# Attention followed by a gated FFN on one Trainium2 core: the two FFN layers interleaved, or in two phases with the gated values kept in DRAM between them

## The chip, the core and the metric

One core of a Trainium2 chip runs the whole kernel. The metric is the device time of one execution in microseconds (us). Engines are TensorE (PE; its weight loads are listed apart as PEld), VectorE (DVE), ScalarE (ACT), GpSimd (POOL) and SyncE (SP), which issues nearly all DMAs and issues them in order.

## What is computed

```python
# q, k, v: [B=4, H=8, S=768, D=64] float32; n_global = 8, n_local = 96
scores = q @ k.T / sqrt(D) + bias        # bias: -slope[head] * distance
scores = where(is_global | is_local, scores, -1e9)   # 8 first keys, 96 keys back
a = exp(scores - max); a = a / (a.sum(-1) + 1e-9)
x = (a @ v).transpose(0, 2, 1, 3).reshape(3072, 512)
h = x @ w_in                             # 512 x 2048
g = h * (1 / (1 + exp(-h)))
out = g @ w_out                          # 2048 x 512
```

The weights w_in and w_out lie in DRAM as float64.

## The kernel before

**Attention.** There are 24 blocks i of 128 query rows (6 per batch), each with 4 head pairs. A block loads k, q and v (L433, 256 KB each) and the 104 keys before it (L440, L443), turns k and q on TensorE (L448), computes the scores (L532 with whole float32 operands in the first 6 blocks, L508 with stacked high and low parts after that), softmax on VectorE and ScalarE (L547, L555, L562 to L571), turns the probabilities (L580), and multiplies them with v (L600, L614). The first blocks turn the result in one step more (L636). x is kept as a high and a low part, xh and xl (L645, L648), so that the FFN's products are three matmuls each: high times high, high times low, low times high.

**The FFN.** Two blocks i make a group g of 256 tokens; there are 12 groups. The hidden width is cut into 16 blocks f of 128. For each g and f:

- `moe_h`, the first layer: 12 matmuls of 128x256 (L763), 3 for each of 4 pieces c of the model width.
- `moe_tanh` on ScalarE (L769) and `moe_gate` on VectorE (L773) make the gated value th, 128x256 in float32. `moe_high` (ScalarE, L777) and `moe_low` (VectorE, L781) split it into gh and gl.
- `moe_o`, the second layer: 6 matmuls of 128x512 (L788), 3 for each of 2 token tiles tt, added up over the 16 f in one PSUM bank for each tt. After the last f, `moe_end` (L798, L800) halves the sum into osb and `moe_out` (L806) stores it.

**The weights.** 32 tiles n, each 512 KB of float64, alternate: n even is w_in for block f = n/2, n odd w_out for the same f. `stage` loads one, three VectorE steps (`conv1` to `conv3`, L368, L374, L380) put a float32 together out of the two words, ScalarE rounds it to the high part (`conv_hi`, L387), and VectorE subtracts (`conv_lo`, L391). All 32 tiles stay in SBUF in both parts (WIH, WIL, WOH, WOL, the last two of w_out in w_last); while those two are not yet filled they serve as staging buffers for eight of the loads (`lent`).

**The exponent scan.** All 32 tiles are loaded a second time (`stage` with the name c), and `check` reduces the exponents of each to a least and a greatest value (L411, two reductions for each tile). At the end they and a few other conditions are judged (`judge`, `verdict`, `keep`), and where one fails a general kernel runs after the fast one. A scan's load waits until four reductions before it are done, and for a first-layer block of the FFN: block 34 + 4n, counted over all groups.

**What sets the order.** Each operation is entered in a planner (`Plan`, L48 to L167) with its engine, an expected cost, a rank, what it depends on and which buffers it takes. `run` simulates all engines and lets each, whenever it is free, take the operation of the lowest rank that is ready and has room in the buffers. The order in which the operations were taken is then written out as the program of each engine, and nothing is reordered afterwards. PSUM's 8 banks are shared out by kind: at any time a table `own` in `room` keeps some banks for each kind, and `hold` says which of its three rows applies. `PAR` (L29 to L39) holds the costs and ranks. Where the planner has TensorE idle within its first 60 us (`WEND`=60000 ns), it puts in a filler: one matmul of 128x256 on a tile of zeros, whose result nobody uses (L899). For the ranks: attention's head pair u = 4i + hp has rank u; a weight tile has C0 + CR·n, its load LW less; all FFN matmuls have ranks over 1000, so that they fill up what attention leaves. In the order that results the second layer of group g stands between the first-layer blocks of group g + 1, one `moe_o` for each `moe_h`, from the start to the end.

Of the kernel before, what the change touches and what calls it, by code (L numbers as in the profile page):

```python
# [10 lines left out]
F32 = mybir.dt.float32  # L11
# [36 lines left out]
class Plan:  # L48
# [122 lines left out]
def attn_moe(ctx, tc, q, k, v, n_global, n_local, w_in, w_out, out):  # L171
# [23 lines left out]
    psum = ctx.enter_context(tc.tile_pool(name="psum", bufs=1, space=PSUM))  # L195

# [5 lines left out]
    NLAST = 2  # L202
    WOH = const.tile([P, NFC - NLAST, DM], F32R, name="WOH")
    WOL = const.tile([P, NFC - NLAST, DM], F32R, name="WOL")
    last_w = []

    def w_o(i, f):

        if f < NFC - NLAST:
            return (WOH, WOL)[i][:, f]  # L210
        if not last_w:
            last_w.extend(
                const.tile([P, NLAST, DM], F32R, name=f"w_last{x}", tag=f"last{x}") for x in range(2)
            )
        return last_w[i][:, f - (NFC - NLAST)]
# [76 lines left out]
    def bias_of(first, hp):  # L292
# [17 lines left out]
        big=3, qkn=3, vn=2, vp=2, KH=2, KL=2, QH=2, QL=2, pe=3, pt=2, xh=2, xl=2, mid=3, th=2, gh=2, gl=2,  # L310
# [34 lines left out]
    def weights(n, parts=True):  # L345

        f, o = divmod(n, 2)
        fs = slice(f * P, (f + 1) * P)
        if o:
            src = w_out.bitcast(U32).rearrange("(c p) (m w) -> c p m w", p=P, w=2)[f]  # L350
            return (src, w_o(0, f), w_o(1, f)) if parts else (src,)
        src = w_in.bitcast(U32).rearrange("(c p) (f w) -> p c f w", p=P, w=2)[:, :, fs]
        return src, WIH[:, :, fs], WIL[:, :, fs]

    def lent(n):
        return n % 5 - 3 if n < PAR["NX"] and n % 5 > 2 else None

    def stage(n, nm):
        if nm == "w" and lent(n) is not None:
            x = const.tile([P, 512, 2], U32, name=f"wl_{n}", tag=f"last{lent(n)}")  # L360
        else:
            x = sb3.tile([P, 512, 2], U32, name=f"{nm}_{n}", tag="big")
        st[nm, n] = x
        nc.sync.dma_start(x if n % 2 else x.rearrange("p (c f) w -> p c f w", c=NCC), weights(n, False)[0])

    def conv1(n):
        st["f", n] = f = sb2.tile([P, 512], U32, name=f"wf_{n}", tag="mid", bufs=5)
# [10 lines left out]
    def conv3(n):  # L378
        f = st["f", n]
        nc.vector.scalar_tensor_tensor(  # L380
            f, st["w", n][..., 1], 0xC0000000, f, ALU.bitwise_and, ALU.bitwise_or
        )
        f = f.bitcast(F32)
        st["f", n] = f if n % 2 else f.rearrange("p (c f) -> p c f", c=NCC)

    def conv_hi(n):
        nc.scalar.copy(weights(n)[1], st["f", n])  # L387

    def conv_lo(n):
        _, hi, lo = weights(n)  # L390
        nc.vector.tensor_sub(lo, st["f", n], hi.bitcast(F32))  # L391

    o_w, o_l = [], [None, None]
    for n in range(2 * NFC):
        rank = PAR["C0"] + PAR["CR"] * n
        a, m, x = [] if lent(n) is not None else [Buf("big")], Buf("mid"), lent(n)
        o = op("DMA", 1456, rank - PAR["LW"], (lambda n=n: stage(n, "w")), [o_l[x]] if not a else (), a, PAR["DW"])
        o = op("DVE", 335, rank, (lambda n=n: conv1(n)), [o], [*a, m])
        o = op("DVE", 602, rank, (lambda n=n: conv2(n)), [o], [*a, m])
        o = op("DVE", 602, rank, (lambda n=n: conv3(n)), [o], [*a, m])  # L400
        if x is not None:
            o_l[x] = o
        o_wf = o
# [252 lines left out]
    for i in range(B * NJ):  # L656
# [12 lines left out]
        for nm in "kq" if i else "":  # L669
# [97 lines left out]
    def moe_tanh(g, f):  # L767
        mo["th", g, f] = th = sb2.tile([P, GT], F32, name="th")
        nc.scalar.activation(th, mo["ph", g, f], AF.Tanh, scale=0.5)  # L769
# [4 lines left out]

    def moe_high(g, f):
        mo["gh", g, f] = gh = sb2.tile([P, GT], F32R, name="gh")
        nc.scalar.copy(gh, mo["th", g, f])  # L777

    def moe_low(g, f):
        mo["gl", g, f] = gl = sb2.tile([P, GT], F32R, name="gl")  # L780
        nc.vector.tensor_sub(gl, mo["th", g, f], mo["gh", g, f].bitcast(F32))  # L781

    def moe_o(g, f, tt, po):
        gh, gl, po = mo["gh", g, f], mo["gl", g, f], bank(po)
# [23 lines left out]
    o_h = {}  # L808
    FIRST = -1e6
    for g in range(NGRP):  # L810
        po = [Buf("po"), Buf("po")]
        last = [None, None]
        o = o_h[g - 1, NFC - 1] if g > 1 else None
        for f in range(NFC):
            rank = 1e3 + (max(g, 1) * NFC + f + (PAR["LAG"] + 0.5 if g else 0))
            ph, th, gh, gl = Buf("h"), Buf("th"), Buf("gh"), Buf("gl")
            for c in range(NCC):
                o = op("PE", 329, rank + PAR["LK"] / 10, (lambda g=g, f=f, c=c, h=ph: moe_h(g, f, c, h)),
                       [o, *o_w[2 * f]] + o_x[g], [ph, xb[g]["xh"], xb[g]["xl"]])
                if f == c == 0:  # L820
                    o["hold"] = 2 if g == 1 else 1
            o_h[g, f] = o
            t = op("ACT", 264, FIRST + rank, (lambda g=g, f=f: moe_tanh(g, f)), [o], [ph, th])
            t = op("DVE", 335, FIRST + rank, (lambda g=g, f=f: moe_gate(g, f)), [t], [ph, th])
            hi = op("ACT", 307, FIRST + rank, (lambda g=g, f=f: moe_high(g, f)), [t], [th, gh])
            lo = op("DVE", 335, FIRST + rank, (lambda g=g, f=f: moe_low(g, f)), [hi], [th, gh, gl])
            for tt in range(NB):
                last[tt] = op("PE", 651, rank, (lambda g=g, f=f, tt=tt, x=po[tt]: moe_o(g, f, tt, x)),
                              [hi, lo, last[tt], *o_w[2 * f + 1]], [gh, gl, *po[tt:]])
                if g < 2 and f == NFC - 1:  # L830
                    last[tt]["hold"] = 1
        ob = Buf("big")
        for tt in range(NB):
            parts = (0, 1) if g == NGRP - 1 and tt == NB - 1 else (None,)
            for h in parts:
                eng = "ACT" if tt % 2 and not h else "DVE"
                o = op(eng, dict(ACT=478, DVE=598)[eng] // len(parts), FIRST + rank,
# [4 lines left out]
    for u, o in o_s.items():  # L842
        g, m = divmod(u, NB * NHP)
        f = (g - 1) * NFC + m * NFC // (NB * NHP) - PAR["AHEAD"]
        if f >= 2 * NFC:
# [229 lines left out]
```

## Time and profile before

| | |
|---|---|
| two runs | 725.86 and 727.01 us, median 726.43 |
| span of the profiled execution | 724.9 us |
| DMA packets | 117499, 63.95 MB, mean 88 GB/s |
| HBM read, written | 56.69 MB, 6.29 MB |
| TensorE clock granted, by 40 slices of the span | 9 tenths or more in each |

The profile is of one execution. The span runs from the first to the last instruction of the program; the run's own device time is not shown for that execution, so the table sets the span beside the two runs. The busy time of TensorE counts matmuls that overlap, since the next one starts before the one ahead has ended; what a matmul costs in a dense row is the distance from its start to the next one's start. Rows of grouped instructions name the line, the engine, the operation, output and inputs, and after the bar the busy time, the mean of one in ns, and the idle time of the engine just before them with what ended most of it.

### The profile page before, as it was taken

The page shows a single profiled execution, that of the slowest core. Times are in us where ns is not written, and L with a number is a line of the kernel's source. Part 1 is how long each engine was busy: PE and PEld are TensorE (multiplying, and loading weights), DVE is VectorE, ACT ScalarE, POOL GpSimd, SP SyncE. Part 2 cuts the span into 40 slices and gives each one's busy share as a digit, 9 for nine tenths or more (in the row PEclk, how much of TensorE's full clock was granted, in tenths as well). Part 3 has the DMA queues.
Part 4 walks back from the last instruction along what each step waited for, and adds up shares of the span by engine and source line. Part 5 has one row for each costly group of instructions (what it writes and reads, how often), then busy time and mean ns, then how long its engine had stood idle before and what let it go on. Part 6 is the DMA issues. An engine that isn't in the chain of part 4 may idle for free.

```text
span 724.9 us, 13945 instructions
## 1 busy us (share of the span) xinstructions
PE 715.0 (99%) x5142; PEld 640.5 (88%) x5142; DVE 463.5 (64%) x1403; ACT 420.6 (58%) x1105; POOL 24.9 (3%) x81
## 2 busy tenths in 40 slices
PE   8999999999999999999999999999999999999996
PEld 5889899888999999998999999999899989998995
DVE  3599999767666667466666665665766666543332
ACT  5897444587557567566565565664755655543321
POOL 2000000000000000000000000000000000000000
PEclk9999999999999999999999999999999999999999
DMA  7888645043225123143142240421422412000000
GB/s 154 214 240 247 192 131 172 2 117 101 59 57 143 45 71 97 48 114 103 30 114 81 64 114 23 122 72 44 132 59 57 127 32 57 30 1 1 30 1 33
DMA packets 117499, 63.95 MB, mean 88 GB/s; under 512 B 93744, under 2 KB 110384, under 8 KB 117424
## 3 DMA queue, kind: packets, MB, share of 16 engines
q1 hardware_dynamic: 116992, 62.86, 32.2%
q8 instruction: 42, 0.69, 0.4%
q14 instruction: 33, 0.27, 0.1%
q10 hardware_dynamic: 432, 0.13, 0.1%
HBM read 56.69 MB, written 6.29 MB: 87 GB/s over the span
## 4 chain that ended last, share of the span: by engine, by line
PE 97%; DVE 1%; DMA 1%; ACT 1%; issue 0%; SPq 0%; ACTq 0%
PE bank L763 38%; PE bank L788 37%; PE bank L580 5%; PE bank L600 4%; PE bank L508 4%; PE bank L448 3%; PE bank L614 3%; PE bank L532 2%; DMA qn<-in_q_dram 1%; PE bank L899 0%; PE bank L636 0%; ACT pe L555 0%; DVE osb L800 0%; ACT osb L798 0%; DVE xl L648 0%
## 5 line engine op out<-in xcount | busy, mean ns | idle before, releaser
L763 PE MATMUL bank<-xh,WIH 128*128 128x256 f32 x768 | 223.6, 291 | 0.0
L763 PE MATMUL bank<-xl,WIH 128*128 128x256 f32 x768 | 216.2, 282 | 0.3 <-DVE xl L648 0.3
L763 PE MATMUL bank<-xh,WIL 128*128 128x256 f32 x768 | 214.8, 280 | 0.0
L763 PEld LDWEIGHTS bank<-xh,WIH 128*128 128x128 f32 x768 | 144.5, 188 | 9.8 <-issue 2.8
L763 PEld LDWEIGHTS bank<-xl,WIH 128*128 128x128 f32 x768 | 144.6, 188 | 6.8 <-DVE xl L648 0.5
L763 PEld LDWEIGHTS bank<-xh,WIL 128*128 128x128 f32 x768 | 144.8, 189 | 0.0
L788 PE MATMUL bank<-WOH,gh 128*128 128x512 f32 x336 | 135.9, 405 | 0.0
L777 ACT CAST gh<-th 128x256 fp32r<-128x256 f32 x192 | 77.3, 403 | 96.0 <-PE bank L788 68.6
L788 PE MATMUL bank<-WOH,gl 128*128 128x512 f32 x336 | 132.4, 394 | 0.0
L788 PE MATMUL bank<-WOL,gh 128*128 128x512 f32 x336 | 131.9, 393 | 0.0
L769 ACT ACTIVATE th<-bank 128x256 f32<-128x256 f32 x192 | 73.8, 384 | 94.4 <-PE bank L763 83.2
L773 DVE SCALAR_TENSOR_TENSOR th<-th,bank 128x256 f32<-128x256 f32 x192 | 80.5, 419 | 60.9 <-ACT th L769 59.1
L781 DVE TENSOR_TENSOR gl<-th,gh 128x256 fp32r<-128x256 f32 x192 | 81.5, 425 | 55.9 <-ACT gh L777 52.7
L547 DVE CUSTOM_DVE_ANT_0 pe<-bank,B 128x232 f32<-128x232 f32 (+1 forms) x192 | 69.0, 377 | 67.2 <-PE bank L508 55.7
L555 ACT ACTIVATE pe<-pe,NM 128x232 f32<-128x232 f32 (+1 forms) x192 | 90.2, 471 | 20.3 <-DVE NM L547 18.8
L586 ACT COPY pt<-bank 128x512 f32<-128x512 f32 (+1 forms) x96 | 52.6, 549 | 46.9 <-PE bank L580 46.8
L788 PEld LDWEIGHTS bank<-WOH,gl 128*128 128x128 f32 x336 | 63.0, 188 | 15.2
L788 PEld LDWEIGHTS bank<-WOL,gh 128*128 128x128 f32 x336 | 63.4, 189 | 6.3
L788 PEld LDWEIGHTS bank<-WOH,gh 128*128 128x128 f32 x336 | 63.4, 189 | 6.3 <-issue 0.3
L580 PE MATMUL bank<-ident,pe 128*128 128x128 f32 (+1 forms) x352 | 54.3, 274 | 0.6 <-DVE pe L571 0.6
L580 PEld LDWEIGHTS bank<-ident,pe 128*128 128x128 f32 (+1 forms) x352 | 42.0, 138 | 7.3 <-ACT xh L645 0.8
L411 DVE TENSOR_REDUCE TOP<-c 128x1 f32<-128x512 int16 x64 | 42.3, 680 | 0.4 <-DMA c<-in_moe_w_in_dram 0.4
(115 smaller groups left out, 899.2 us busy)
## 6 DMA issues: line engine op xcount, KB each, us to landing
c<-in_moe_w_in_dram SPq DMA_DIRECT2D x16, 512.0 KB, 4.7
c<-in_moe_w_out_dram SPq DMA_DIRECT2D x16, 512.0 KB, 4.7
vn<-in_v_dram SPq DMA_DIRECT2D x24, 256.0 KB, 4.0
w<-in_moe_w_in_dram SPq DMA_DIRECT2D x12, 512.0 KB, 4.4
w<-in_moe_w_out_dram SPq DMA_DIRECT2D x12, 512.0 KB, 4.2
kn<-in_k_dram SPq DMA_DIRECT2D x23, 256.0 KB, 3.0
qn<-in_q_dram SPq DMA_DIRECT2D x23, 256.0 KB, 3.1
out_dram<-osb SPq DMA_DIRECT2D x23, 256.0 KB, 3.1
```

What stands on the lines that cost most here:

```text
L411: nc.vector.tensor_reduce(TOP[:, i, n:n + 1], top, AX.X, (ALU.min, ALU.max)[i], apply_absolute_value=True)
L508: nc.tensor.matmul(ps[:, a, :n], t[x][:, hp], t[K[a]][:, hp, w0:], start=not m, stop=m == 1)
L547: nc.vector.tensor_tensor_reduce(t["p", hp][:, a, :n], t["s", hp][a][:, :n], B1[:, h] if i % NJ else B0[:, h], -SC, 3.0e38, ALU.add, ALU.m ...
L555: nc.scalar.activation(x, x, AF.Exp, bias=NM[:, i * H + h:i * H + h + 1], scale=-1.0, accum_out=t["sum", hp][:, a:a + 1],)
L580: nc.tensor.transpose(ps[:n, c, a], pe[:, a, c0:c0 + n], ident)
L586: nc.scalar.copy(t["pt", hp][:, c], t["tp", hp][:, c])
L763: nc.tensor.matmul(ph, w[:, c, fs], x[:, c], start=not c and not n, stop=c == NCC - 1 and n == 2)
L769: nc.scalar.activation(th, mo["ph", g, f], AF.Tanh, scale=0.5)
L773: nc.vector.scalar_tensor_tensor(gf, gf, 1.0, mo["ph", g, f], ALU.add, ALU.mult)
L777: nc.scalar.copy(gh, mo["th", g, f])
L781: nc.vector.tensor_sub(gl, mo["th", g, f], mo["gh", g, f].bitcast(F32))
L788: nc.tensor.matmul(po, a[:, s], w_o(w, f), start=f == 0 and n == 0, stop=f == NFC - 1 and n == 2)
```

## The change

The two layers are split in two loops. In the first, all groups' `moe_h`, tanh and gate are entered, and each gated value, 128 KB, is written to DRAM (`moe_put`, L777, 192 of them on SP's queue). In the second, all groups' `moe_o` follow; their gated values are fetched back, two f at a time (`moe_get`, L781, 256 KB, 96 of them, each let go by the second layer six blocks ahead, GA=6, the first ones by the last blocks of the first layer), and `moe_high` (L785) and `moe_low` (L789) work on two f at once, so 96 of each where there were 192.

With it go:

- Weights: all of w_in first (n < 16), with ranks from 8 on (C0) and loads 12 ahead of that (LW); w_out after it with rank 8 + 5·(n - 16), so spread over the time of attention. The w_in tiles are staged in the buffers of the w_out tiles, which are not yet filled (tags wo0 to wo15): eight for the loads and eight for the float32 words, so a w_in tile from the ninth on waits for the conversion of the one eight before it.
- Scans: a scan's load waits for a second-layer block, 12 + 5n, instead of a first-layer one, so all 32 lie in the second phase.
- PSUM: `own` has other numbers, and the row with hold 2 begins at the second phase. `HU`, the head pair at which row 1 begins, is 9 instead of 13.
- The planner's costs of FFN matmuls are 355 and 700 ns instead of 329 and 651 (for three matmuls each), that of a w_in load 2000 instead of 1456.

```diff
-    CAP=dict(po=4, av=2, s=4, h=3, tp=2, tq=4), HU=13,
-    C0=14, CR=1, LW=1, LB=5, QB=3.5, RI=0.1, RN=0, RP=0.2, RM=0, RV=1.2, RQ=0.1, RB=3, LK=-25, LAG=1,
-    BP=(4, 3), NX=20, CF=2, AHEAD=5, CN=4, I0=6, IV=6, QS='ACT',
+    CAP=dict(po=4, av=2, s=4, h=3, tp=2, tq=4), HU=9,
+    C0=8, CR=1, LW=12, LB=5, QB=3.5, RI=0.1, RN=0, RP=0.2, RM=0, RV=1.2, RQ=0.1, RB=3, LK=-25, LAG=1,
+    BP=(4, 3), CF=12, AHEAD=5, CN=5, I0=6, IV=6, QS='ACT', O0=2, ON=5, GA=6, PF=16,
...
     def stage(n, nm):
-        if nm == "w" and lent(n) is not None:
-            x = const.tile([P, 512, 2], U32, name=f"wl_{n}", tag=f"last{lent(n)}")
+        if nm == "w" and n < NFC:
+            x = const.tile([P, 512, 2], U32, name=f"ws_{n}", tag=f"wo{HF + n % HF}")
...
+    def moe_put(g, f):
+        if g not in gate:
+            gate[g] = dram.tile([P, NFC, GT], F32, name=f"gate{g}")
+        nc.sync.dma_start(gate[g][:, f], mo["th", g, f])
+
+    def moe_get(g, f):
+        mo["g", g, f] = x = sb2.tile([P, 2, GT], F32, name="gx", tag="mid", bufs=5)
+        nc.sync.dma_start(x, gate[g][:, f:f + 2])
+
     def moe_high(g, f):
-        mo["gh", g, f] = gh = sb2.tile([P, GT], F32R, name="gh")
-        nc.scalar.copy(gh, mo["th", g, f])
+        mo["gh", g, f] = gh = sb2.tile([P, 2, GT], F32R, name="gh", tag="QH")
+        nc.scalar.copy(gh, mo["g", g, f])
...
+    for g in range(NGRP):
+        o = o_h[g - 1, NFC - 1] if g else None
+        for f in range(NFC):
+            rank = 1e3 + g * NFC + f
+            ph, th = Buf("h"), Buf("g1")
+            for c in range(NCC):
+                o = op("PE", 355, rank, (lambda g=g, f=f, c=c, h=ph: moe_h(g, f, c, h)),
+                       [o, *o_w[f]] + o_x[g], [ph, xb[g]["xh"], xb[g]["xl"]])
...
+            o_put[g, f] = op("DMA", 364, FIRST + rank, (lambda g=g, f=f: moe_put(g, f)), [t], [th], PAR["DO"])
+
     for g in range(NGRP):
...
-            rank = 1e3 + (max(g, 1) * NFC + f + (PAR["LAG"] + 0.5 if g else 0))
...
+            rank = 1e4 + g * NFC + f
+            if not f % 2:
+                gx = Buf("pt")
+                at = g * NFC + f - PAR["GA"]
+                o_g = op("DMA", 728, rank, (lambda g=g, f=f: moe_get(g, f)),
+                         [o_put[g, f], o_put[g, f + 1], o_h[NGRP - 1, max(at + NFC, 0)] if at < 0 else o_o[at]], [gx], PAR["DL"])
...
     for n, o in enumerate(o_cd):
-        g, f = divmod(2 * NFC + PAR["CF"] + PAR["CN"] * n, NFC)
-        plan.after(o, o_h[g, f])
+        plan.after(o, o_o[PAR["CF"] + PAR["CN"] * n])
```

By the two orders, three places look like this. The first is TensorE around the first FFN matmul. Before, the scores of 15 head pairs (L532, two matmuls each) stand ahead of it, and right before it turns of a block's result (L636) and of probabilities (L580):

```order
L532 MATMUL bank_83<-KHw,QHw 128x232
L532 MATMUL bank_88<-KHw,QHw 128x232
L636 MATMUL bank_82<-ident,xq 128x128 x4
L580 MATMUL bank_87<-ident,pe 104x128 x2
L580 MATMUL bank_87<-ident,pe 128x128 x2
L763 MATMUL bank_84<-xh,WIH 128x256
L763 MATMUL bank_84<-xl,WIH 128x256
L763 MATMUL bank_84<-xh,WIL 128x256
L532 MATMUL bank_85<-KHw,QHw 128x232
```

In the change, with the last of a row of fillers ahead of it (L918 is the old L899, L531 the old L532, L762 the old L763):

```order
L918 LDWEIGHTS wx
L918 MATMUL bank_88<-wx 128x256
L531 MATMUL bank_87<-KHw,QHw 128x232
L531 MATMUL bank_85<-KHw,QHw 128x232
L531 MATMUL bank_82<-KHw,QHw 128x232
L531 MATMUL bank_83<-KHw,QHw 128x232
L762 MATMUL bank_89<-xh,WIH 128x256
L762 MATMUL bank_89<-xl,WIH 128x256
L762 MATMUL bank_89<-xh,WIL 128x256
```

The first FFN matmul has moved ahead of attention's work: the scores of 10 head pairs stand ahead of it, and 56 fillers (27 of 28 before), twelve of them in a row.

The second place is SP's queue from its sixth row on, in the first 10 us. Before, there are only loads for attention:

```order
L433 DMA kn<-in_k_dram 128x8x64
L433 DMA qn<-in_q_dram 128x8x64
L433 DMA vn<-in_v_dram 128x8x64
L440 DMA vp<-in_v_dram 96x8x64
L443 DMA vp<-in_v_dram 8x8x64
```

In the change, weight tiles (ws of w_in, w of w_out, L359) stand among them:

```order
L432 DMA kn<-in_k_dram 128x8x64
L432 DMA qn<-in_q_dram 128x8x64
L359 DMA ws_176<-in_moe_w_in_dram 128x4x256
L359 DMA w_203<-in_moe_w_out_dram 128x1024
L432 DMA vn<-in_v_dram 128x8x64
L439 DMA vp<-in_v_dram 96x8x64
L442 DMA vp<-in_v_dram 8x8x64
L359 DMA ws_263<-in_moe_w_in_dram 128x4x256
```

Two weight tiles have moved ahead of block 1's v, and more ahead of block 2's k and q.

The third place is VectorE where scans stand. Before, a reduction (L411) stands among attention's steps and the gate and difference (L773, L781) of the FFN:

```order
L781 TENSOR_TENSOR gl<-th,gh 128x256
L411 TENSOR_REDUCE TOP<-c_4142 128x1
L562 TENSOR_SCALAR rs<-sm 128x2
L566 RECIPROCAL rs<-rs 128x2
L571 TENSOR_SCALAR pe<-pe,rs 128x232
L773 SCALAR_TENSOR_TENSOR th<-th,bank_82 128x256
```

In the change, where the second phase begins, there are only the reductions (L410), the differences for two f (L789) and the output (L808):

```order
L808 TENSOR_SCALAR osb<-bank_84 128x512
L410 TENSOR_REDUCE TOP<-c_6753 128x1 x2
L789 TENSOR_TENSOR gl<-gx,gh 128x512 x2
L410 TENSOR_REDUCE TOP<-c_6803 128x1
L789 TENSOR_TENSOR gl<-gx,gh 128x512
L410 TENSOR_REDUCE TOP<-c_6803 128x1
L789 TENSOR_TENSOR gl<-gx,gh 128x512 x2
L410 TENSOR_REDUCE TOP<-c_6856 128x1 x2
```

The scans have moved out of attention's time to between the differences on which the second layer's third matmul waits. For every second tile both reductions stand together, for the others one difference lies between them.

More of the change, by code (lines that the diff above doesn't have):

```diff
@@ L195, in attn_moe @@
     psum = ctx.enter_context(tc.tile_pool(name="psum", bufs=1, space=PSUM))
+    dram = ctx.enter_context(tc.tile_pool(name="gates", bufs=1, space=bass.MemoryType.DRAM))
+    gate = {}
     ident = const.tile([P, P], F32, name="ident")
@@ L201, in attn_moe @@
     WIL = const.tile([P, NCC, DFF], F32R, name="WIL")
[L202 to L205, printed above, removed]
+    w_t = {}
     def w_o(i, f):
[L209 to L215, printed above, removed]
+        return w_t[f][:, i]
     NM = const.tile([P, B * NJ * H], F32, name="NM")
@@ L342, in attn_moe, with source, parts @@
             )
-    def weights(n, parts=True):
-        f, o = divmod(n, 2)
-        fs = slice(f * P, (f + 1) * P)
[L349 to L356, printed above, removed]
+    def source(n):
+        o, f = divmod(n, NFC)
+        if o:
+            return w_out.bitcast(U32).rearrange("(c p) (m w) -> c p m w", p=P, w=2)[f]
+        return w_in.bitcast(U32).rearrange("(c p) (f w) -> p c f w", p=P, w=2)[:, :, f * P:(f + 1) * P]
+    def parts(n):
+        o, f = divmod(n, NFC)
+        if o:
+            return w_o(0, f), w_o(1, f)
+        fs = slice(f * P, (f + 1) * P)
+        return WIH[:, :, fs], WIL[:, :, fs]
+    HF = NFC // 2
     def stage(n, nm):
-        if nm == "w" and lent(n) is not None:
-            x = const.tile([P, 512, 2], U32, name=f"wl_{n}", tag=f"last{lent(n)}")
+        if nm == "w" and n < NFC:
+            x = const.tile([P, 512, 2], U32, name=f"ws_{n}", tag=f"wo{HF + n % HF}")
         else:
@@ L806, in moe_out @@
         eng.dma_start(out[n * P:(n + 1) * P, h], mo["out", g][:, tt, h])
-    o_h = {}
+    o_h, o_put, o_o = {}, {}, {}
     FIRST = -1e6
+    for g in range(NGRP):
[6 more added lines that the diff above has]
+                       [o, *o_w[f]] + o_x[g], [ph, xb[g]["xh"], xb[g]["xl"]])
+                if f == c == g == 0:
+                    o["hold"] = 1
+            o_h[g, f] = o
+            t = op("ACT", 264, FIRST + rank, (lambda g=g, f=f: moe_tanh(g, f)), [o], [ph, th])
+            t = op("DVE", 335, FIRST + rank, (lambda g=g, f=f: moe_gate(g, f)), [t], [ph, th])
+            o_put[g, f] = op("DMA", 364, FIRST + rank, (lambda g=g, f=f: moe_put(g, f)), [t], [th], PAR["DO"])
     for g in range(NGRP):
@@ L812, in attn_moe @@
         last = [None, None]
-        o = o_h[g - 1, NFC - 1] if g > 1 else None
         for f in range(NFC):
-            rank = 1e3 + (max(g, 1) * NFC + f + (PAR["LAG"] + 0.5 if g else 0))
[L816 to L826, printed above, removed]
-            for tt in range(NB):
[L828 to L831, printed above, removed]
@@ L832, in attn_moe @@
+            for tt in range(NB):
+                last[tt] = op("PE", 700, rank, (lambda g=g, f=f, tt=tt, x=po[tt]: moe_o(g, f, tt, x)),
+                              [hi, lo, last[tt], *o_w[NFC + f]], [gh, gl, *po[tt:]])
+            o_o[g * NFC + f] = last[1]
+            if not g and not f:
+                last[0]["hold"] = 2
         ob = Buf("big")
         for tt in range(NB):
-            parts = (0, 1) if g == NGRP - 1 and tt == NB - 1 else (None,)
-            for h in parts:
+            parts_ = (0, 1) if g == NGRP - 1 and tt == NB - 1 else (None,)
@@ L836, in attn_moe @@
+            for h in parts_:
                 eng = "ACT" if tt % 2 and not h else "DVE"
-                o = op(eng, dict(ACT=478, DVE=598)[eng] // len(parts), FIRST + rank,
+                o = op(eng, dict(ACT=478, DVE=598)[eng] // len(parts_), FIRST + rank,
                        (lambda g=g, tt=tt, h=h: moe_end(g, tt, h)), [last[tt]], [po[tt], ob])
```

61 lines of the change are left out of this document (34 added, 27 removed).

## The prediction

> **What bounds the kernel now.** I read the page first (busy shares, chain of waits), then TensorE's own waits, then its rows in order of time, and last the windows.
>
> ```profile
> span 724.9 us, 13945 instructions
> PE 715.0 (99%) x5142; PEld 640.5 (88%) x5142; DVE 463.5 (64%) x1403; ACT 420.6 (58%) x1105; POOL 24.9 (3%) x81
> PE 97%; DVE 1%; DMA 1%; ACT 1%; issue 0%; SPq 0%; ACTq 0%
> ```
>
> The third row is the chain that ended last: 97% of the span runs through TensorE. Busy matmul time overlaps itself, so "99%" alone proves little; the waits do. All of TensorE's, in the whole span:
>
> ```profile
> PE bank L899 <- DVE wx L307: 1.1, 1, 1.1
> PE bank L448 <- DMA qn<-in_q_dram: 0.9, 1, 0.9
> PE bank L580 <- DVE pe L571: 0.6, 1, 0.6
> PE bank L448 <- DMA kn<-in_k_dram: 0.6, 1, 0.6
> PE bank L763 <- DVE xl L648: 0.3, 1, 0.3
> ```
>
> Five waits, 3.5 us together, and 2.6 of them are the start, before any q or k has landed. What remains is matmuls back to back, and their price is read from start to start, here where attention is over:
>
> ```profile
> 680.35 0.40 PE L788 MATMUL bank<-WOH,gh 128*128 128x512 f32 x1
> ...
> 681.75 0.28 PE L763 MATMUL bank<-xh,WIH 128*128 128x256 f32 x1
> ...
> 683.17 0.40 PE L788 MATMUL bank<-WOH,gh 128*128 128x512 f32 x1
> ```
>
> Six second-layer matmuls (L788) take 1.40 us, 0.233 each; twelve first-layer ones (L763) 1.42, 0.118 each. The 1152 and 2304 of them make 269 + 273 = 542 us. The windows say whether other engines' load changes that:
>
> ```profile
> 30.00:40.00 10.00, 10.00 (x83) 8.10 (x81) 9.04 (x33) 8.79 (x29) 0.66 (x2) 1.00 0.96 259
> 50.00:60.00 10.00, 10.00 (x82) 8.79 (x81) 9.85 (x30) 8.90 (x27) 0.00 (x0) 1.00 0.96 257
> 250.00:350.00 100.00, 100.00 (x745) 90.63 (x744) 65.66 (x204) 62.61 (x162) 2.52 (x8) 1.00 0.34 92
> 680.00:700.00 20.00, 20.00 (x131) 18.11 (x130) 5.94 (x14) 5.54 (x14) 0.00 (x0) 1.00 0.00 1
> ```
>
> Columns are length, then busy time of PE, PEld, DVE, ACT, POOL, the granted clock, DMA share, GB/s. With DVE at 98% and ACT at 89% (50 to 60), or both under 30% (680 to 700), TensorE stays full. So TensorE's instruction count sets the time, and a reordering can gain only the 3.5 us of waits and the start.
>
> [...]
>
> **The change, part by part.** The counts of the real matmuls are the same in both orders (2304 first-layer, 1152 second-layer, 264 + 88 value, 352 transpose), so the 542 us and attention's share stay.
>
> 1. Fillers. The order has 56 of them (L899, now L918) where it had 28, all within its first 171 rows. Both orders agree up to the third of the three at 15.20; after that the before has 7 more and the change 35. They run whether or not TensorE has anything to wait for:
>
> ```profile
> 9.34 1.25 PE L899 MATMUL bank<-wx 128*128 128x256 bf16 x5
> 10.52 0.80 PE L532 MATMUL bank<-KHw,QHw 64*128 64x128 f32 x4
> ...
> 21.22 0.49 PE L899 MATMUL bank<-wx 128*128 128x256 bf16 x3
> 21.55 0.60 PE L636 MATMUL bank<-ident,xq 128*128 128x128 f32 x4
> ...
> 41.52 0.37 PE L763 MATMUL bank<-xh,WIH 128*128 128x256 f32 x1
> ```
>
> Five take 1.18 us early (0.24 each), three take 0.33 at 21 us (0.11 each). The 28 more are late ones: 28 x 0.11 = +3.1 us. Ends: 0, if each stands where TensorE would have waited anyway, and 28 x 0.24 = 6.6. I take 3.1, since TensorE's list of waits has nothing between 6 and 158 us that they could cover.
>
> 2. First-layer work starts earlier: by the order some 12 us of attention matmuls and the 35 fillers (3.9) lie between 15.5 and the first L762, so about 32 us instead of 41.52. That gains nothing by itself: TensorE was full from 20 to 41 us with attention, which is only moved behind.
>
> 3. The wait where attention resumes. The before stops attention for most of 60 to 140 us and has this when it starts again:
>
> ```profile
> 159.18 0.43 PE L580 MATMUL bank<-ident,pe 128*128 128x128 f32 x2 [0.63 <-DVE pe L571]
> 160.01 0.39 PE L763 MATMUL bank<-xl,WIH 128*128 128x256 f32 x1 [0.27 <-DVE xl L648]
> ```
>
> The change never stops attention: -0.9 us (ends -0.9 and 0, if the switch to the stacked scores waits in the same way).
>
> 4. Weight tiles of the first layer. All sixteen are needed by the end of group 0, the last at about 76 us (32, plus 45 us of matmuls that the order has up to there). By SP's order 16.2 MB land up to it: 8.4 of w_in, 1.6 of w_out, 1.4 of gates, 4.8 of attention's tiles.
>
> ```profile
> 0.00:10.00 10.00, 7.40 (x33) 4.56 (x34) 3.95 (x22) 4.49 (x14) 3.08 (x13) 1.00 0.65 137
> 20.00:30.00 10.00, 10.00 (x89) 9.44 (x91) 4.17 (x17) 9.14 (x28) 0.72 (x2) 1.00 0.87 223
> w<-in_moe_w_in_dram SPq DMA_DIRECT2D x12, 512.0 KB, 4.4
> L391 DVE TENSOR_TENSOR WIL<-wf,WIH 128x512 fp32r<-128x512 f32 x16 | 11.0, 688 | 0.0
> ```
>
> 1.4 MB by 10 us at the first row's rate, and the rest at the 257 GB/s of 50 to 60, make 68 us; four DVE steps (three like the L391 row, one shorter), ACT's cast and the hops add about 3.5: 71.5 against 76. At the second row's 223 it is 76.4 + 3.5, 4 us late. Puts add a coupling: SP issues in order, so every k, q, v or weight load behind a put waits until that gate is computed. Ends 0 and 4; I take 0.5, by the higher rate, which was held from 30 to 60 us.
>
> 5. Attention beside first layers alone. The page's ACT and DVE busy time, less what leaves this phase:
>
> ```profile
> L777 ACT CAST gh<-th 128x256 fp32r<-128x256 f32 x192 | 77.3, 403 | 96.0 <-PE bank L788 68.6
> L781 DVE TENSOR_TENSOR gl<-th,gh 128x256 fp32r<-128x256 f32 x192 | 81.5, 425 | 55.9 <-ACT gh L777 52.7
> L411 DVE TENSOR_REDUCE TOP<-c 128x1 f32<-128x512 int16 x64 | 42.3, 680 | 0.4 <-DMA c<-in_moe_w_in_dram 0.4
> ```
>
> ACT 420.6 - 77.3 = 343 and DVE 463.5 - 81.5 - 42.3 = 340 us over about 449 us (724.9 less 269 less the tail): 76% each, against 63 and 66% in the window from 250 to 350. The window from 50 to 60 had more on both and no wait. Ends: 0, and a wait like the 0.63 at 159.18 in each of 18 later blocks, 11 us. I take 0.3.
>
> 6. Spill and fetch. A put is 128 KB beside the load of 256 KB that lands in about 3 us; six th tiles at one per 1.42 us leave 8.5 us for tanh, gate and put. A get is issued six hidden blocks ahead of its use, so it has five, 7.0 us, for landing, cast (0.6) and difference (0.69).
>
> ```profile
> kn<-in_k_dram SPq DMA_DIRECT2D x23, 256.0 KB, 3.0
> out_dram<-osb SPq DMA_DIRECT2D x23, 256.0 KB, 3.1
> ```
>
> 7.0 against 3.1 + 1.3: hidden, and 25 MB each way bring the second phase to about 180 GB/s (25 gets, 17 scans, 6 outputs in 269 us), under the 257 seen. If the cover failed, every one of the 96 pairs would pay. At the phase change the first gets leave while group 11's last five first-layer blocks run (7 us). Taken: 0.
>
> 7. The exponent scans (c tiles) move from attention's time into the second phase, where DVE does little else, and stand in front of the gl that TensorE needs next.
>
> ```profile
> DMA to landing us min/median/max: 4.1/4.7/5.3
> ```
>
> For the odd tiles, gl is wanted four hidden blocks (5.6 us) and two matmuls (0.47) after the scan's load is let go; 6.07 less one scan (0.68), gl (0.69) and a hop of 0.1 leaves 4.6 to land in. The even ones have one block more and two scans, 5.3, but a get is issued first (0.4). At 4.1 nothing waits, at 4.7 it is 16 x 0.1 = 1.6 us, at 5.3 16 x 0.7 + 16 x 0.4 = 17.6. I take 0.5, since the L411 row has 0.4 us of idle for 64 scans.
>
> The end, from the last matmul at 718.07 to 724.9, has the same instructions.
>
> ```profile
> 718.07 0.40 PE L788 MATMUL bank<-w_last,gl 128*128 128x512 f32 x1
> ```
>
> **Sum**: 724.9 + 3.1 - 0.9 + 0.5 + 0.3 + 0.5 = 728.4 us of span. The median of the runs shown, 726.43, is 1.5 above this execution's span; with that, 729.9 us, 0.5% over the before.
>
> **The rivals.** (a) *The fillers are free.* They replace idle time that TensorE would have had in this order, and the wait at 159 goes: 726.43 - 0.9 = 725.5. For it: the order was made by a planner that puts a filler only where it foresees idleness. Against: its DMA cost for a first-layer tile is 2000 ns, while 0.5 MB at 257 GB/s is as much only when the queue is full.
> (b) *Late weight tiles.* Parts 4 and 5 fall to their upper halves, through SP's queue held by puts: 4 and 3 in place of 0.8, about 736. For it: 71.5 against 76 us is a small margin. Against: DMA share 0.96 was held from 30 to 60 us.
> (c) *Slower: scans block gl.* In the second phase DVE is in order, so a scan whose tile has not landed holds the gl behind it. It decides from a landing of 4.6 us; at 5.3 it is 729.9 - 0.5 + 17.6 = 747. For it: 180 GB/s instead of 92 in the windows. Against: the 0.4 us of idle in the L411 row, and that a load not queued behind others is quicker.
> (d) *Second layers alone run quicker.* If mixing costs spacing, a pure phase could fall from 0.233 to the length of a weight load, one per matmul:
>
> ```profile
> L788 PEld LDWEIGHTS bank<-WOH,gl 128*128 128x128 f32 x336 | 63.0, 188 | 15.2
> ```
>
> 1152 x (0.233 - 0.188) = 52 us, so 678 at the very best. Against: six in a row between first layers cost just what the rows above show, and no first or last one stands out. [...]
>
> **How the numbers follow.** Forecast 0.6, (a) 0.14, (b) 0.14, (c) 0.09, (d) 0.03. A kernel measured here can be told from no change at about 2%, 14.5 us: under 711.9 is (d) alone, 0.03; over 740.9 is (c) and a bad case of (b) or part 5, 0.09; the rest, 0.88, is within. The range reaches from a little under (a), 724, to 740, below (c): some 0.85 inside, and no wider than parts 4, 5 and 7 make it.
>
> **What would show it.** L918 in 56 rows with no wait near them, first L762 near 32 us, L762 in group 0 without waits for WIL; TensorE's list of waits still a few us; the second phase 269 us long with six per 1.40 us; no wait for gl behind L410. I am wrong if the list of waits grows beyond some 10 us, if the second phase is much longer or shorter than 269 us, or if the first 60 us hold less work than now.

## The result

The changed kernel took 735.06 us in the median of two runs (734.54 to 735.57), where the one before took 726.43: 1.0116 of it, 95% interval 1.0087 to 1.0146. Five more runs beside the experiments gave 737.38 against 726.40, 1.0147 (1.0134 to 1.0161). The forecast was 729.9 with a range of 724 to 740: the side and the range hold, and the loss is 9 to 11 us instead of 3.5. By the 2% that the prediction sets as its mark this is no change; both intervals, however, lie wholly above 1. The profiled execution took 735.57 us, its span 733.3.

### The profile page after: what moved, and what is told of

The parts are those of the page before. It is cut to its first block, busy times and chain, and to the rows that moved or that the text cites. A ratio compares the mean times of both kernels' runs of the same rounds, so it can differ in the third digit from the quotient of the medians.

```text
span 733.3 us, 14421 instructions
## 1 busy us (share of the span) xinstructions
PE 721.6 (98%) x5170; PEld 649.0 (89%) x5170; DVE 452.2 (62%) x1307; ACT 398.1 (54%) x1009; POOL 28.9 (4%) x81
## 4 chain that ended last, share of the span: by engine, by line
PE 82%; DVE 11%; DMA 2%; ACT 2%; issue 2%; SPq 0%; ACTq 0%
PE bank L796 37%; PE bank L762 30%; PE bank L599 4%; PE bank L579 4%; PE bank L507 4%; PE bank L447 2%; DVE pe L546 2%; DVE wf L373 1%; DVE wf L379 1%; DVE th L772 1%; DVE wf L367 1%; DMA kn<-in_k_dram 1%; DVE WIL L392 1%; PE bank L531 1%; ACT pe L554 1%
## 5 line engine op out<-in xcount | busy, mean ns | idle before, releaser
L796 PE MATMUL bank<-wo,gh 128*128 128x512 f32 x768 | 241.6, 396 | 0.0
L762 PE MATMUL bank<-xh,WIH 128*128 128x256 f32 x768 | 226.5, 295 | 0.0
L762 PE MATMUL bank<-xh,WIL 128*128 128x256 f32 x768 | 216.0, 281 | 0.0
L762 PE MATMUL bank<-xl,WIH 128*128 128x256 f32 x768 | 215.7, 281 | 0.0
L796 PEld LDWEIGHTS bank<-wo,gh 128*128 128x128 f32 x768 | 144.1, 188 | 34.7
L785 ACT CAST gh<-gx 128x512 fp32r<-128x512 f32 x96 | 59.6, 620 | 174.6 <-PE bank L796 170.4
L796 PE MATMUL bank<-wo,gl 128*128 128x512 f32 x384 | 151.9, 396 | 0.0
L762 PEld LDWEIGHTS bank<-xh,WIH 128*128 128x128 f32 x768 | 145.1, 189 | 4.7 <-issue 4.1
L789 DVE TENSOR_TENSOR gl<-gx,gh 128x512 fp32r<-128x512 f32 x96 | 66.5, 692 | 129.8 <-ACT gh L785 129.7
L762 PEld LDWEIGHTS bank<-xl,WIH 128*128 128x128 f32 x768 | 145.2, 189 | 0.0
L762 PEld LDWEIGHTS bank<-xh,WIL 128*128 128x128 f32 x768 | 144.7, 188 | 0.1
L796 PEld LDWEIGHTS bank<-wo,gl 128*128 128x128 f32 x384 | 72.1, 188 | 17.5
L410 DVE TENSOR_REDUCE TOP<-c 128x1 f32<-128x512 int16 x64 | 42.1, 679 | 13.5 <-DMA c<-in_moe_w_in_dram 6.8
L561 DVE TENSOR_SCALAR rs<-sm 128x2 f32<-128x2 f32 x72 | 12.4, 173 | 51.7 <-ACT pe L554 51.2
L579 PEld LDWEIGHTS bank<-ident,pe 128*128 128x128 f32 (+1 forms) x352 | 40.4, 137 | 3.9 <-DVE pe L570 1.2
L570 DVE TENSOR_SCALAR pe<-pe,rs 128x232 f32<-128x232 f32 (+1 forms) x144 | 42.0, 331 | 1.3
```

The costliest lines, as they stand in the source:

```text
L410: nc.vector.tensor_reduce(TOP[:, i, n:n + 1], top, AX.X, (ALU.min, ALU.max)[i], apply_absolute_value=True)
L570: nc.vector.tensor_scalar(x, x, t["inv", hp][:, a:a + 1], None, ALU.mult)
L579: nc.tensor.transpose(ps[:n, c, a], pe[:, a, c0:c0 + n], ident)
L762: nc.tensor.matmul(ph, w[:, c, fs], x[:, c], start=not c and not n, stop=c == NCC - 1 and n == 2)
L785: nc.scalar.copy(gh, mo["g", g, f])
L789: nc.vector.tensor_sub(gl, mo["g", g, f], mo["gh", g, f].bitcast(F32))
```

## The profile after the change

The page's span, busy shares and chain of waits:

```profile
span 733.3 us, 14421 instructions
PE 721.6 (98%) x5170; PEld 649.0 (89%) x5170; DVE 452.2 (62%) x1307; ACT 398.1 (54%) x1009; POOL 28.9 (4%) x81
PE 82%; DVE 11%; DMA 2%; ACT 2%; issue 2%; SPq 0%; ACTq 0%
```

VectorE has less to do than before (452 us instead of 463), and yet 11% of the chain, 80 us, now runs through it, where it was 1%. TensorE's own waits, all of them:

```profile
PE bank L447 <- DMA kn<-in_k_dram: 2.0, 2, 1.4
PE bank L918 <- DVE wx L299: 1.1, 1, 1.1
PE bank L447 <- DMA qn<-in_q_dram: 0.9, 1, 0.9
PE bank L613 <- ACT pt L585: 0.7, 1, 0.7
PE bank L579 <- DVE pe L570: 0.5, 1, 0.5
PE bank L635 <- DVE xq L629: 0.2, 1, 0.2
```

The first three were there before, but for 1.4 us of the k load. So the list grew from 3.5 to 5.4 us and explains 2 of the 8.4 us by which the span grew. TensorE also runs 28 fillers more, 3.1 us at 0.11 each; whether they cost that is tested below. Where the time is lost, the windows say (length, then busy time of PE, PEld, DVE, ACT, POOL, clock, DMA share, GB/s):

```profile
20.00:40.00 20.00, 19.95 (x176) 18.17 (x173) 19.86 (x58) 16.28 (x49) 1.48 (x3) 1.00 0.74 192
40.00:60.00 20.00, 20.00 (x173) 19.14 (x173) 19.86 (x51) 14.66 (x38) 0.72 (x2) 1.00 0.89 239
60.00:80.00 20.00, 17.91 (x147) 16.51 (x146) 19.79 (x48) 12.70 (x33) 2.57 (x1) 1.00 0.89 249
80.00:100.00 20.00, 19.81 (x161) 18.18 (x159) 15.18 (x40) 14.66 (x36) 0.00 (x0) 1.00 0.90 233
```

VectorE is full from 20 to 80 us, and TensorE first looks full too (part of it is fillers) and then, from 60 on, stands idle for 2.1 us. The chain, asked for in this stretch (start, length, what), shows what VectorE does there and what follows:

```profile
61.37 0.60 DVE WIL L392
61.97 0.60 DVE wf L373
...
67.29 0.60 DVE wf L379
...
70.39 7.07 DMA kn<-in_k_dram
```

Conversions of weight tiles (wf, WIL) follow each other up to 67 us. Then comes a k load of 256 KB that takes 7.07 us where the k loads of the kernel before take 3.0 in the median, behind what SP issued in the 3.3 us ahead of it, three tiles of 512 KB and a put:

```profile
67.06 0.44 SPq L359 DMA_DIRECT2D ws<-in_moe_w_in_dram  x1
68.59 0.33 SPq L777 DMA_DIRECT2D gate<-th  x1
69.36 0.38 SPq L359 DMA_DIRECT2D ws<-in_moe_w_in_dram  x1
69.79 0.49 SPq L359 DMA_DIRECT2D w<-in_moe_w_out_dram  x1
70.39 0.38 SPq L432 DMA_DIRECT2D kn<-in_k_dram  x1
```

On TensorE these are the two waits:

```profile
66.59 1.07 PE L579 MATMUL bank<-ident,pe 128*104 128x128 f32 x8
68.39 0.43 PE L613 MATMUL bank<-vp,pt 104*128 104x64 f32 x2 [0.73 <-ACT pt L585]
...
75.88 0.28 PE L762 MATMUL bank<-xh,WIL 128*128 128x256 f32 x1
77.50 0.65 PE L447 MATMUL bank<-ident,kn 128*128 128x128 f32 x4 [1.35 <-DMA kn<-in_k_dram]
```

One later piece stands for what the first phase still loses: FFN matmuls in a row, and then a turn of probabilities that are not normed yet.

```profile
149.85 0.28 PE L762 MATMUL bank<-xh,WIL 128*128 128x256 f32 x1
150.65 0.57 PE L579 MATMUL bank<-ident,pe 128*104 128x128 f32 x2 [0.52 <-DVE pe L570]
```

The second phase, beginning at 457.9 us, has none of it:

```profile
600.00 0.63 PE L796 MATMUL bank<-wo,gh 128*128 128x512 f32 x2
600.47 0.40 PE L796 MATMUL bank<-wo,gl 128*128 128x512 f32 x1
600.70 0.63 PE L796 MATMUL bank<-wo,gh 128*128 128x512 f32 x2
```

Three matmuls in 0.70 us: 0.233 each, as in the prediction's rows of the mixed layers; its 1152 take 268.87 us.

## The experiments

The medians are over four to six runs each (e8: eleven), beside runs of the kernel before, which took 726.71 us (e1 to e4), 726.40 (e5 to e8), 726.78 (e9 to e11) and 726.16 (e12). To tell a stretch's share from what differs between executions at the start (last section), the traces (one execution of each kernel) are also compared by stages, whose ends are starts of matmuls: A from the row of three fillers at 14 to 15.5 us to group 1's first layer, B from there to group 2's, C to group 4's, D to the second phase, E to the last matmul.

| us | A | B | C | D | E | sum |
|---|---|---|---|---|---|---|
| before | | | | | | 702.9 |
| the change | 66.3 | 37.8 | 72.7 | 266.0 | 268.9 | 711.6 |
| e1 fewer fillers | 66.7 | 37.7 | 72.7 | 266.0 | 269.1 | 712.2 |
| e3 puts on GpSimd's queue | 67.5 | 37.9 | 71.8 | 265.8 | 268.9 | 712.0 |
| e4 w_out later | 62.9 | 37.4 | 72.6 | 265.9 | 268.9 | 707.7 |
| e9 light w_in | 64.8 | 37.5 | 72.7 | 266.0 | 268.9 | 709.8 |
| e10 light w_out | 65.2 | 37.6 | 70.2 | 266.0 | 269.3 | 708.2 |
| e11 both light | 63.9 | 37.5 | 70.2 | 266.0 | 268.9 | 706.3 |

Theory A is that VectorE's weight conversions set the pace of the first stretch; theory B is the prediction's, that a filler costs its 0.11 us.

**e1: fewer fillers.**

```diff
     def filler(b):
-        nc.tensor.matmul(bank(b, 2 * P), warm[:, :P], warm, start=True, stop=True)
+        fills.append(b)
+        if len(fills) <= 21 or b not in fills[:-1]:
+            nc.tensor.matmul(bank(b, 2 * P), warm[:, :P], warm, start=True, stop=True)
```

> The changed kernel with 32 of its 56 fillers left out (24 stay: the first 21, which run up to 15.5 us, and three that are the first matmul on their bank); nothing else is moved. Theory A, formed from the trace of the change: from 20 to 70 us its chain of waits runs through DVE, which is 98 to 100% busy there with converting weight tiles, and then through the k load of 70.39 that lands at 77.5. Then TensorE's fillers lie in time that it would have waited, and leaving them out only makes the waits at 67 and 76 us longer: 735 (734 to 735.5), with TensorE's list of waits 3 us longer. Theory B, that of the prediction: a filler costs its 0.11 us wherever TensorE does not wait next to it: 32 x 0.11 = 3.5 us less, 731.5.

736.75 us (735.33 to 737.15), ratio 1.0130 (1.0115 to 1.0146): not below the change's first 735.06, and 0.6 below its 737.38, inside the spread. Of 3.5 us nothing clear came back, because new waits took their place, at three spots of TensorE's list:

```profile
PE bank L447 <- DMA kn<-in_k_dram: 2.3, 2, 1.6
PE bank L613 <- ACT pt L585: 1.2, 2, 0.7
PE bank L531 <- ACT QHw L510: 1.1, 1, 1.1
```

Theory B falls for this kernel: TensorE was ahead of VectorE, and the fillers stood in time that it would have waited.

**e2: the same fillers in the kernel before.**

```diff
+        fills.append(b)
+        for _ in range(29 if len(fills) == 27 else 1):
             nc.tensor.matmul(bank(b, 2 * P), warm[:, :P], warm, start=True, stop=True)
```

> The kernel before, with 28 more fillers in one row at 38 us, where its TensorE was dense. The same two theories on the other kernel. B: 28 x 0.109 = 3.1 us more, 729.5. A would give this too if the kernel before is bound by TensorE there, and about 726.5 (no change) if it, too, hangs on DVE (99% busy from 50 to 60 us) up to 60 us. A result between them says how much of the 3.1 us is covered.

730.87 us (729.79 to 731.07), 4.2 more than before. In its trace the row is paid in full:

```profile
39.19 3.33 PE L903 MATMUL bank<-wx 128*128 128x256 bf16 x29
42.35 0.33 PE L614 MATMUL bank<-vp,pt 104*128 104x64 f32 x2
```

29 in 3.16 us, 3.05 for the 28 more, and nothing behind it gets shorter. The other 1.05 us of this execution come from its start (last section). So the price of the prediction was right for the kernel before, whose chain runs through TensorE for 97%.

**e3: puts on GpSimd's queue.**

```diff
     def moe_put(g, f):
...
-        nc.sync.dma_start(gate[g][:, f], mo["th", g, f])
+        nc.gpsimd.dma_start(gate[g][:, f], mo["th", g, f])
```

> The changed kernel with its 192 puts issued on GpSimd's queue; gets, loads and everything else stay on SP. Theory C: the puts on SP's queue hold the loads behind them until a gate is computed (SP sat 10.7 us before one of them at 70 us), so the k load that TensorE waited 1.4 us for comes too late: then the waits at 76 us and some after it go, 732 to 733.5. Theory A: DVE and the full DMA queue set the pace up to 77 us, not SP's order: 734.5 to 735.5. If GpSimd issues more slowly than SP, a put can also come late and hold a gate's buffer: above 736.

736.43 us (735.40 to 737.74). The k wait of 1.4 us went as theory C has it, and others came:

```profile
PE bank L762 <- DVE WIL L392: 1.6, 2, 1.1
PE bank L531 <- POOL KHw L520: 1.1, 1, 1.1
```

TensorE now waits for the conversion itself (WIL), and once for a copy of keys that GpSimd made late (KHw, 1.1 us), so e3 brings a delay of its own. What settles theory C is the last w_in tile. In e3 its load is issued at 51.21 us (the last of the three in the first row) instead of 69.36, and VectorE begins to convert it no sooner; the second and third rows are the change's and e3's, the last is TensorE in e3:

```profile
50.04 2.48 SPq L359 DMA_DIRECT2D ws<-in_moe_w_in_dram  x3
75.28 0.43 DVE L367 TENSOR_SCALAR wf<-ws 128x512 uint32<-128x512 uint32 x1
75.31 0.42 DVE L367 TENSOR_SCALAR wf<-ws 128x512 uint32<-128x512 uint32 x1
80.64 0.38 PE L762 MATMUL bank<-xh,WIL 128*128 128x256 f32 x1 [1.07 <-DVE WIL L392]
```

So here the order of SP's queue decided which wait is seen (1.4 us for k in the change, 1.6 for WIL in e3), and VectorE's conversions how long the stretch is (the last tile from 75.28 or 75.31 us on). Theory C falls.

**e4: w_out's conversions later, fewer fillers.**

```diff
-    ... I0=6, IV=6, QS='ACT', O0=2, ON=5, GA=6, PF=16,
+    ... I0=6, IV=6, QS='ACT', O0=8, ON=5, GA=6, PF=16,
```

and the filler edit of e1 (24 fillers are left here too, not the 21 of the expectation).

> The changed kernel with the w_out tiles' ranks from 32 on instead of 8 (O0 = 8), so that their loads and conversions begin after most of w_in's, and with 21 fillers only. Theory A: three to four w_out tiles, 2.2 us of DVE each, leave the stretch from 20 to 77 us, in which DVE is the chain, and 2 MB leave the queue ahead of the k load: the waits at 67 and 76 us go, and with them the cover of the fillers, which are left out here: 735 - 3.5 - 2.4 = 729. Theory B: 731.3 from the fillers alone. If neither holds (the loss sits after 80 us), 734 to 735.

732.75 us (731.51 to 733.93), ratio 1.0085 (1.0070 to 1.0101): 4.0 less than e1, which has the filler edit too. Of the 4.5 us by the stages, 3.8 are in stage A (66.7 to 62.9). Its chain and its window from 60 to 80:

```profile
PE 88%; ACT 5%; DVE 4%; DMA 1%; issue 1%; SPq 0%; ACTq 0%
60.00:80.00 20.00, 20.00 (x173) 19.90 (x172) 14.19 (x33) 10.92 (x30) 0.00 (x0) 1.00 0.85 224
```

VectorE's share of the chain fell from 11% to 4%, and TensorE is full from 60 to 80. The 729 of theory A was not reached: something else is left. The edit also takes 2 MB of loads out of the stretch, so by itself it does not tell VectorE's load from the queue's; e9 to e11 do.

**e5: the change again.** The changed kernel without an edit.

> The changed kernel itself once more, five rounds beside the kernel before on the chip that also runs the next three: 735.1 by the first measurement, which had two runs. If it is 736 to 737, the run with fewer fillers (736.75 on another chip) was no slower than the change; if it is 735, leaving the fillers out cost something.

737.38 us (735.50 to 738.45). Its trace has the change's stages to within 0.2 us, so leaving the fillers out (e1) cost nothing clear either.

**e6: no scans.**

```diff
+    nc.vector.memset(TOP, 16000.0)
...
-    for n in range(2 * NFC):
+    for n in range(0):
         a = Buf("big")
```

> The changed kernel with the 32 exponent scans left out (their loads and 64 reductions; the table that is judged is filled with a constant), so this leaves part of the check of the weights out. The order of all work up to the second phase is the same. Theory A (the loss lies in the first phase, above all from 20 to 80 us): no change against the changed kernel, 735 to 736. Theory D: the second phase's 16.8 MB of scan loads and the reductions cost: its matmuls have 233.3 ns from start to start where the dense stretches of before have 232.0, so 1152 x 1.3 ns = 1.5 us less, 733.5; and more if gl is held anywhere.

735.49 us (734.22 to 735.93), 1.9 less than e5. That is the size that theory D named, but not in its place: in the traces the second phase takes 268.9 us with scans and 268.6 without, and the 1.0 us by which this execution is ahead of the change's is there at 14 us already (last section). Its window beside the change's, in the second phase (the first row is the change's):

```profile
460.00:560.00 100.00, 100.00 (x430) 80.54 (x429) 42.01 (x64) 24.32 (x40) 0.00 (x0) 1.00 0.60 195
```

```profile
460.00:560.00 100.00, 100.00 (x430) 80.53 (x429) 27.74 (x40) 23.94 (x40) 0.00 (x0) 1.00 0.40 124
```

430 matmuls in 100 us in both, with 195 GB/s or 124, VectorE at 42% or 28%. The scans cost 0.3 us there at most, where theory D has 1.5. Theory D falls; without the trace the medians would have spoken for it.

**e7: more margin.** As e4, with MG2=800.

> As in e4 (w_out tiles from rank 32 on, 24 fillers), and the margin that the planner adds after 45 us to whatever TensorE takes over from another engine raised from 400 to 800 ns (MG2), so that FFN matmuls go ahead of a turn of probabilities that would only just be ready. What is left of the loss in e4 (6.0 us against before) is by theory E the short waits of TensorE for probabilities (L579) and scores between 120 and 200 us, some 2.5 us: these go, 730. Theory F: the rest is spacing and switching between kinds of matmul, which a margin does not change, or later work is only moved: 732.5 or more.

734.85 us (731.38 to 735.79; two runs at 731.4 and 732.0, one of them profiled, and four from 734.8 on), not less than e4. The turns are late all the same, for instance:

```profile
160.73 0.28 PE L762 MATMUL bank<-xh,WIL 128*128 128x256 f32 x1
161.36 0.79 PE L579 MATMUL bank<-ident,pe 128*104 128x128 f32 x4 [0.35 <-DVE pe L570]
```

The margin moved the turn and did not make VectorE's norm (L570) earlier: TensorE waits 0.35 us for it here. Theory F's number came out, which says little about its reason.

**e8: the kernel before with fewer fillers.** The filler edit of e1 in the kernel before.

> The kernel before with 21 of its 28 fillers, the 7 that run after 15.5 us left out. By the price of 4.2 us for 28 more (e2), 7 x 0.15 = 1.0 us less, 725.7. If they stand where TensorE would have waited anyway, 726.7.

726.51 us (725.74 to 728.08), ratio 1.0001 (0.9992 to 1.0009). From the three fillers to the last matmul it takes 703.0 us, before 702.9: the seven late ones of the kernel before were free as well. A filler put by the planner is not one put in by hand (e2).

**e9: light w_in.**

```diff
     def conv2(n):
         f = st["f", n]
+        if n < NFC:
+            return
```

with the same in conv3, conv1 with a mask that keeps the values small, and the filler edit of e1.

> As e1 (the order of the change with 24 fillers, 736.75), with two of the three VectorE steps that put a w_in tile's float32 together left out (so the weights' values are wrong and the output with them): 16 x 1.2 = 19 us less of VectorE's time between 14 and 78 us, every other instruction in its place. Theory A (VectorE's conversions set the pace from 20 to 77 us): the waits between 20 and 77 us go, some 5 us: 731.5. Theory G (the k load that takes 7 us from 70.39 on, behind four weight tiles and a put on SP's queue, sets it): the wait at 76 us stays, and the gain is under 1.5 us: 735.5.

733.18 us (732.98 to 734.81), 3.6 less than e1 (2.4 by the stages), between A (731.5) and G (735.5). Stage A gains 1.9. The k load is still waited for, as G has it: with VectorE lighter the DMA queue is next, and VectorE itself is idle for 1.4 us ahead of each of the last two w_in tiles, until its load lands. Its window from 60 to 80:

```profile
60.00:80.00 20.00, 18.20 (x150) 16.82 (x149) 13.54 (x37) 12.36 (x33) 0.00 (x0) 1.00 0.91 240
```

**e10: light w_out.** The same edit with `n >= NFC`.

> As e9, with the two steps left out for the w_out tiles instead: 19 us less of VectorE's time, spread from 20 to 120 us, four tiles' 4.8 us of it before 77. Theory A: about as e4, which moved these tiles away, minus what e4 got from the queue: 733 to 734; and 1 us less if the waits for probabilities from 93 to 170 us are VectorE's too.

732.45 us (731.35 to 732.67), 4.3 less than e1: 1.4 in stage A and 2.5 in stage C, where w_in's tiles are long done and w_out's still run. The window of the change from 120 to 160 us, and that of e10:

```profile
120.00:160.00 40.00, 39.39 (x349) 37.36 (x348) 37.69 (x123) 32.03 (x87) 3.41 (x10) 1.00 0.59 171
```

```profile
120.00:160.00 40.00, 40.00 (x366) 39.26 (x365) 32.76 (x115) 34.35 (x91) 4.42 (x12) 1.00 0.66 182
```

TensorE is full with VectorE at 82% (32.76 of 40), and was not at 94%. So the late probabilities of 120 to 190 us were held by w_out's conversions, the last of which runs at 171 us in the change, not before 120 as the expectation has it.

**e11: both light.** The edit for all n.

> As e9, with the two steps left out for all 32 tiles: 38 us less of VectorE's time, all before 120 us. If VectorE's conversions in the first phase are the whole of the loss, 727 to 728 (what is left is spacing, 1 us, and switches between kinds of matmul). If the waits for probabilities after 120 us have another cause (two engines in turn, with no tile to convert any more), 729.5 to 731.

730.35 us (729.74 to 732.97), ratio 1.0056 (1.0041 to 1.0071): 6.4 less than e1. Stage C is as in e10, so the part of the expectation that gives the waits after 120 us another cause is refuted, though its number came out. What is left against before, 3.6 us, lies in stage A and in small pieces:

```profile
20.00:40.00 20.00, 18.32 (x152) 16.41 (x151) 13.80 (x45) 15.93 (x47) 0.72 (x2) 1.00 0.84 218
40.00:60.00 20.00, 20.00 (x173) 19.14 (x172) 14.63 (x41) 15.16 (x40) 1.27 (x3) 1.00 0.88 251
60.00:80.00 20.00, 19.09 (x157) 17.70 (x156) 11.70 (x32) 12.65 (x34) 0.00 (x0) 1.00 0.94 246
```

TensorE loses 2.6 us here with VectorE at 67%; in its list of waits there are 0.7 us for the k load, 0.8 for a turned q (QHw), 0.7 for turned probabilities (pt) and 0.3 for a result (xq). QHw and pt come from ScalarE, which is busy for 8.55 of the 10 us from 20 to 30, VectorE for 6.41. The light tiles still take two of their four steps on VectorE, so what is left is not free of VectorE either.

**e12: q and k one head pair earlier.** As e4, with QB=4.5.

> As e4 (w_out tiles from rank 32 on, 24 fillers), with the k and q of each block loaded and turned one head pair earlier (QB 3.5 to 4.5): the correct version of the two-phase kernel that the runs so far point to. By theory A, VectorE's conversions from 20 to 60 us still hold the first blocks, whose waits in e4 (0.3 at 22, 0.6 at 28, 0.3 at 30 us) may go at best: 731 to 733, no faster than before (726.7). If the q and k loads were what is left of the loss, 729 or less.

732.30 us (731.31 to 732.66), as e4. No version of the two phases that was tried beats the kernel before.

## Why the prediction was half right

**The side came out by a term that failed.** Of the 3.5 us forecast, 3.1 were fillers, which cost nothing here. Without them the sum gives 726.8, 0.4 above the before; that the loss was on the forecast side and inside the range is in good part luck.

**What held.** In the second phase TensorE's instruction count sets the time; up to some 190 us it does not, and there the premise that the count sets the time failed. The earlier start of the first layer gained nothing by itself: part 2's first L762 came at 31.92 us and brought nothing. Parts 6 and 7 held: spill, fetch and scans are hidden (268.87 us for the second phase, and e6). Rival (d) fell: in a phase of its own a second-layer matmul took 0.2336 us, the mean of 1151 distances, and not the 0.188 of a weight load.

**Part 1, the fillers: right size, wrong place.** Each takes 0.11 us (e2), but leaving 32 out of the change gave nothing clear (e1). The step that failed is its reason, "TensorE's list of waits has nothing between 6 and 158 us that they could cover": that list was the kernel before's. The change made its own waits there, and the fillers filled part of them. Rival (a) was right about the fillers and wrong about the sum.

**Part 3, the wait where attention resumes:** not gained. The change has the like of it at 150 us (0.52), and others up to 190.

**Part 4, the weight tiles: the term that was mis-sized.** 0.5 us was taken, because the last tile would be converted at 71.5 us and needed at 76. In the change it was converted at 80.09, and the matmul that needs its low part started at 80.14; the second tile had been 10 us early. The prediction counts VectorE's conversion for the last tile alone (within its 3.5 us). What counts is VectorE's capacity: a tile takes it 2.5 us (0.42, and three steps of 0.69), the 19 tiles that are done by then 47 us, with attention's work beside them, and it was full from 20 to 80 us. So the last tiles came just in time, and probabilities, k and, in e3, the tiles themselves were waited for in turn. The price is some 4 us: e4 brings 3.8 back in stage A by moving w_out's tiles out of it, e11 2.8 with every load in place. The difference may be the 2 MB of loads or the order that e4 changes too; the runs do not tell these apart. The step that misled was reading the row of 50 to 60 us of before, "DVE at 98%" and TensorE full, as proof that a full VectorE does no harm. In the kernel before it was full up to 100 us:

```profile
60.00:80.00 20.00, 20.00 (x143) 18.23 (x142) 19.84 (x42) 11.74 (x27) 0.00 (x0) 1.00 0.77 217
80.00:100.00 20.00, 20.00 (x129) 18.01 (x128) 19.87 (x43) 9.86 (x22) 0.00 (x0) 1.00 0.46 133
```

But there TensorE had FFN work of groups 0 and 1 in hand (18.6 us of it from 60 to 80), and attention had all but stopped: of its turns of probabilities (L580) 8 stand between 60 and 80 us and none from there to 140. In the change the same conversions stand beside attention, whose every head pair goes through VectorE several times. A full VectorE beside attention was not a wait at once: from 40 to 60 us TensorE had none in either kernel, with VectorE busy for 19.66 of 20 us before and 19.86 in the change.

**Part 5, attention beside first layers:** 0.3 was taken, 2.5 measured (stage C, e10), by w_out's conversions. The estimate of 76% of VectorE spread them evenly over the phase; from 120 to 160 us it was 94%.

**The rivals.** (b) gave the closest number, 736, and the closest place, and the last weight tiles were indeed only just in time. But its mechanism, puts that hold SP's queue, is refuted by e3: with the loads up to 18 us earlier the last tile was converted no sooner. (c) did not occur.

**What is open.** The 3.6 us by which e11 is still slower. Two things in the traces bear on it. Its list of waits sums to 5.1 us, 1.6 more than before. And second-layer matmuls in a row stand 233.3 ns apart in the second phase, where the kernel before has 232.0 (704 distances); over 1148 distances that is 1.5 us. It is the same without scans (e6: 430 matmuls in 100 us as well), so they are not the reason, and none was found.

## What to carry to other kernels

Here a full VectorE beside a full TensorE did no harm where the work that TensorE had in hand did not come from it (20.00 of 20 us from 60 to 80 in the kernel before), and in time it did where that work came from it (17.91 in the change): ask, for each stretch, whose output the next matmuls need, and count that engine's load in the stretch, not over the phase. The 32 fillers that the planner put where it foresaw idle time showed in the count of instructions and not in the time (e1): leave such a filler out and look. When work moves out of a stretch, ask what slack it gave to the others there.

## What was not expected

**The start of an execution decided up to 2 us.** TensorE's matmuls had half their later rate up to a point that differed between executions, though the clock in the rows of the windows was 1.00 before that point too (0 to 10 us, in the prediction). The change turns q (L447) at half rate, 213 ns apart:

```profile
13.44 1.12 PE L447 MATMUL bank<-ident,qn 128*128 128x128 f32 x4
14.35 0.73 PE L613 MATMUL bank<-vn,pt 128*128 128x64 f32 x4
```

and e6 the same four (there L448) 109 ns apart, since its rate had risen by 12.6 us:

```profile
12.99 0.66 PE L448 MATMUL bank<-ident,qn 128*128 128x128 f32 x4
13.48 0.56 PE L614 MATMUL bank<-vn,pt 128*128 128x64 f32 x4
```

Over the profiles of this study the point lies between 12.1 us (e9) and 16 us or later (e2, whose row of three fillers at 15.53 is still at half rate). By that row e6 is 1.0 us ahead of the change (14.10 us against 15.14). The scores that the kernel before computes at 37.52 us (L532) stand at 38.56 in e2, 1.0 us later. Together that is 2 us between an early and a late execution. It is as much as many of the differences looked for here, and the reason for comparing stages behind that point. What sets the point was not shown.

**A put issued by GpSimd took its time.** In e3 the 192 puts took 105.3 us of GpSimd, 548 ns each (SP issues one in 0.33 us in the rows above), which it had to spare but for one late copy of keys (the 1.1 us for KHw).
